# Two parts of the value weights split ahead of the copies of the transposed rows

## Chip, cores and metric

The kernel runs on one core of a Trainium2 chip. The metric is the device time of one execution in microseconds (us); the number given is the median of several executions, with the lowest and the highest beside it.

## What is computed

The input is a matrix of 2048 rows and 512 columns. Four layers follow each other, A, B, A, B. Each one normalizes its rows, projects them with weights of 512 by 512, applies an attention of 32 heads, projects the result back and adds it to its input. The change lies in the first layer A, at the very beginning of the program. Of its reference this matters:

```python
def _layernorm(x, axis=-1, eps=1e-5):
    m = jnp.mean(x, axis=axis, keepdims=True)
    v = jnp.var(x, axis=axis, keepdims=True)
    return (x - m) / jnp.sqrt(v + eps)
...
qkv = (x @ wqkv).reshape(B, S, 3, H, Dh)          # transposed to q, k, v
...
pq = jnp.einsum("bhsd,hdf->bhsf", q, w_phi)
pk = jnp.einsum("bhsd,hdf->bhsf", k, w_phi)
...
kv = jnp.einsum("bhsf,bhsd->bhfd", phi_k, v)
...
x = x + _A_ref(_layernorm(x, axis=-1), A_wqkv, A_w_phi, A_wo)
```

## The kernel before

**Splitting.** A float32 matrix is multiplied in three products of a faster type (fp32r). Each operand is cast to a high half (an ACT copy into a tile of type fp32r), and the low half is what the cast lost (a subtraction, raw minus high). A product is then high x high + high x low + low x high, three matmuls for each of the four parts of 128 that the inner dimension of 512 is cut into (`kc` = 0 to 3). `mm3` (L433) issues them, so one block of 128 rows by 512 columns takes 12 matmuls. In the profile, `w` is a tile of split weights (high or low), `hh` and `hl` are the high and low halves of the normalized and transposed rows, and `P` (tag P4) holds raw weights as loaded.

**The start.** `LayerA.first` (L648) works on the first 512 rows (four tiles of 128 rows, `t` = 0 to 3). It loads the raw key weights, the four row tiles, the raw value weights and the raw query weights, in this order, on SP's queue (`fetch`, L253, and `rows_of`, L393). While these land, PE transposes the key weights and folds `w_phi` into them (`folded`, L274). DVE takes the moments of the rows, and ACT and DVE normalize the tiles (L680 to L683): tiles 0 and 2 on ACT (`normal`), tiles 1 and 3 on DVE.

**The place of the change.** Then come, for each row tile, `columns` (L384): four PE transposes into a PSUM buffer of the tag g, an ACT copy to `hh`, and a DVE subtraction to `hl`. The tag g has four buffers (G = 4) that are taken in turn. After these, `next(upc[1])` issues the loads of the next 512 rows on SP into the four row tiles, which the transposes must have read. After that, for each part of the value weights, ACT casts the raw part to `vh` and `low` subtracts it on DVE (parts 0 and 2) or on POOL (parts 1 and 3). The same for the key weights follows, with all four subtractions on DVE. Then `v_tile` (L536) makes the values of the first row tiles: twelve matmuls for tile 0, twelve for tile 1, then the sixteen transposes of the query weights, then tiles 2 and 3.

```python
for t in range(4):
    columns(hT, t, xt[t])
upc = upcoming(1)
next(upc[1])
for kc in range(NC):
    act.copy(vh[:, kc, :], vraw[kc])
    low(pool if kc % 2 else dve, wv, kc, vraw[kc])
```

**What sets the order.** Each engine runs its instructions in order. The class `Ordered` (L144) ties every instruction of DVE, ACT, POOL and SP to the one written before it, and `held` (L164) does so for PE, so the program text is the order. An exception is marked by `loose`: the instructions of `prepare` (L297), which splits the weights of the later layers piece by piece and stores them, are tied to what stands before them, but nothing is tied to them. `run(p1[0], prepare())` (L1508) takes turns between the first pass of layer 1 and this preparation; `first` is run through before the preparation issues anything. Nearly all instructions carry the line of a helper (L154 for DVE, ACT, POOL and SP, L176 for matmuls, L180 for transposes), so they are told apart by the names of their tiles.

Of the kernel before, what the change touches and what calls it, by code (L numbers as in the profile page):

```python
# [20 lines left out]
NC = D // P  # L21
# [79 lines left out]
def interleave_kernel(ctx, tc, x_in, a_wqkv, a_wphi, a_wo, b_wq, b_wk, b_wv, b_wo, b_beta,  # L101
# [13 lines left out]
    def nm(s):  # L115
        uid[0] += 1
        return f"{s}_{uid[0]}"

    def T2(tag, bufs, dt=F32, shape=(P, 512)):
        return sp.tile(list(shape), dt, tag=tag, bufs=bufs, name=nm(tag))  # L120
# [41 lines left out]
    dve, act, pool, sync = [Ordered(e) for e in (nc.vector, nc.scalar, nc.gpsimd, nc.sync)]  # L162
# [51 lines left out]
    def wtiles(tag):  # L214
        if tag == "e8":
            return [T2("e8", 2 * NSET, F32R, (P, NC, D)) for _ in range(2)]
        return [wp.tile([P, NC, D], F32R, tag="w8", name=nm("w")) for _ in range(2)]

    def dtile(shape, name):
        return dr.tile(list(shape), F32, name=name)  # L220
# [32 lines left out]
    def fetch(src):  # L253

        raw = []
        for a in range(2):
            t = T2("P4", NP4, shape=(P, 2, D))
            sync.dma_start(out=t, in_=src[2 * a * P : 2 * (a + 1) * P, :].rearrange("(k p) n -> p k n", p=P))
            raw += [t[:, 0, :], t[:, 1, :]]
        return raw  # L260
# [13 lines left out]
    def folded(raw, chunks):  # L274


        wT = T2("e8", 2 * NSET, shape=(P, NC, D))
        for kc in range(NC):
            pt = PS("g", G)
            for c in range(NC):  # L280
                tp(pt[:, c * P : (c + 1) * P], raw[kc][:, c * P : (c + 1) * P], ident)
            act.copy(wT[:, :, kc * P : (kc + 1) * P], pt.rearrange("p (c x) -> p c x", c=NC))
            yield
        pf = PS("lg", 1, (P, 2, 512))
        pf = [pf[:, 0], pf[:, 1], PS("mx", 1), PS("my", 1)]
        for kc in range(NC):
            chunks.append(pf[kc])
            for c in range(NC):
                mm(chunks[kc][:, c * P : (c + 1) * P], lhsT=wT[:, c, kc * P : (kc + 1) * P],
                   rhs=phibd[:, c].rearrange("p h f -> p (h f)"), start=True, stop=True)  # L290
        yield
# [67 lines left out]
    def moments(st, t, x):  # L359
        bs = T2("bs", 2, shape=(P, 6))  # L360
        dve.bn_stats(bs, x)
        dve.bn_aggr(st[:, t, 0:2], bs)

    def guard(st):
        dve.tensor_scalar(st[:, :, 1], st[:, :, 1], 1e-5, None, op0=ADD)

    def root(st):
        act.activation(st[:, :, 3], st[:, :, 1], AF.Ln)
        act.activation(st[:, :, 2], st[:, :, 3], AF.Exp, scale=-0.5)

    def refine(st, eng):

        var, r, u = st[:, :, 1], st[:, :, 2], st[:, :, 3]
        eng.tensor_tensor(out=u, in0=r, in1=r, op=MUL)
        eng.tensor_tensor(out=u, in0=u, in1=var, op=MUL)
        eng.tensor_scalar(u, u, -0.5, 1.5, op0=MUL, op1=ADD)
        eng.tensor_tensor(out=r, in0=r, in1=u, op=MUL)
        eng.tensor_tensor(out=u, in0=st[:, :, 0], in1=r, op=MUL)
        eng.tensor_scalar(u, u, -1.0, None, op0=MUL)

    def normal(st, t, x):
        act.activation(x, x, AF.Identity, bias=st[:, t, 3:4], scale=st[:, t, 2:3])

    def columns(hT, t, x):  # L384
        pt = PS("g", G)
        for kc in range(NC):
            tp(pt[:, kc * P : (kc + 1) * P], x[:, kc * P : (kc + 1) * P], ident)
        pv = pt.rearrange("p (k t) -> p k t", k=NC)
        hv, lv = [h[:, :, t * P : (t + 1) * P] for h in hT]
        act.copy(hv, pv)  # L390
        wait(lambda: dve.tensor_tensor(out=lv, in0=pv, in1=hv.bitcast(F32), op=SUB))

    def rows_of(xsrc, s):  # L393
        xt = []
        for t in range(4):
            x = T2("x", 4)
            sync.dma_start(out=x, in_=xsrc[4 * s + t])
            xt.append(x)
        return xt

    def htiles(spare=None):
        if spare:
            return wtiles(spare)
        return [hp_.tile([P, NC, D], F32R, tag=tag, bufs=1, name=nm(tag)) for tag in ("hh", "hl")]
# [43 lines left out]
    def mm3_pair(one, two, kcs=range(NC), closed=True):  # L448

        terms = [(kc, a, b) for kc in kcs for a, b in ((0, 0), (0, 1), (1, 0))]  # L450
        half = len(terms) // 2
        parts = [(terms[:half], (one, two)), (terms, (two, one)), (terms[half:], (one, two))]
        steps = [(*term, sides, n == 0) for part, sides in parts for n, term in enumerate(part)]
        for step, (kc, a, b, sides, first) in enumerate(steps):
            ends = step == 0, step == len(steps) - 1
            for row, (po, lhs, rhs) in zip((0, 64), sides):
                i = mm(po, lhsT=lhs(a, kc)[row : row + 64], rhs=rhs(b, kc)[row : row + 64],
                       start=ends[0], stop=ends[1] and closed, tile_position=(row, 0))
                if first and step > 0 and row == 0:
                    after(i, passed)  # L460
            if step + 1 < len(steps) and steps[step + 1][4]:
                passed = sync.nop(nofuse=True)
                after(passed, i)
            if not ends[1]:
                yield
# [177 lines left out]
    class LayerA:  # L643
# [4 lines left out]
        def first(self, hT, vv, upcoming):  # L648

            wph = T2("U", 2)[:, 0 : NC * DH].rearrange("p (c f) -> p c f", c=NC)  # L650
            act.dma_start(out=ident, in_=c_ident)
            act.dma_start(out=bd, in_=c_bd)
            act.dma_start(out=wph, in_=a_wphi.rearrange("(c h) d f -> (h d) c f", c=NC))
            nc.scalar.preload_act_table_set("natural_log_exp_and_others")
            kraw = fetch(a_wqkv[:, D : 2 * D])
            xt = rows_of(self.xsrc, SEGS[0])
            vraw, qraw = [fetch(a_wqkv[:, i * D : (i + 1) * D]) for i in (2, 0)]
            st = T2("st", 2, shape=(P, 4, 8))
            hT[:] = htiles()
            (vh, vl), (kh, kl), (qh, ql) = wv, wk, wq = [wtiles(tag) for tag in ("w8", "w8", "e8")]  # L660
            for key, w in (("awv", wv), ("awk", wk), ("awq", wq)):
                kept[key] = [dtile((P, NC, D), nm(key)) for _ in range(2)]
                owed.extend(zip(kept[key], w))

            def low(eng, w, kc, raw):
                eng.tensor_tensor(out=w[1][:, kc, :], in0=raw, in1=w[0][:, kc, :].bitcast(F32), op=SUB)

            for c in range(NC):
                pool.tensor_tensor(out=phibd[:, c], in0=wph[:, c, :].unsqueeze(1).broadcast_to([P, 8, DH]),
                                        in1=bd[:, 16:24].unsqueeze(2).broadcast_to([P, 8, DH]), op=MUL)  # L670
            kf, qf = [], []
            kfold, qfold = folded(kraw, kf), folded(qraw, qf)
            for t in range(4):
                next(kfold)
                moments(st, t, xt[t])
            guard(st)
            root(st)
            refine(st, dve)
            next(kfold)
            normal(st, 0, xt[0])  # L680
            for t in (1, 3):
                dve.tensor_scalar(xt[t], xt[t], st[:, t, 2:3], st[:, t, 3:4], op0=MUL, op1=ADD)
            normal(st, 2, xt[2])  # L683
            for t in range(4):
                columns(hT, t, xt[t])
            upc = upcoming(1)
            next(upc[1])
            for kc in range(NC):
                act.copy(vh[:, kc, :], vraw[kc])
                low(pool if kc % 2 else dve, wv, kc, vraw[kc])  # L690
            for kc in range(NC):
                act.copy(kh[:, kc, :], kf[kc])
                low(dve, wk, kc, kf[kc])
            vt = v_tile(hT, wv, vv, ("g", G))
            for t in range(4):
                for _ in range(4):
                    next(vt)
                if t == 1:
                    for _ in range(4):
                        next(qfold)  # L700
                for _ in range(NEXT[t]):
                    next(upc[1])
            next(qfold)
            for kc in range(NC):
                act.copy(qh[:, kc, :], qf[kc])
                low(dve, wq, kc, qf[kc])
            return wq, wk, wv, upc
# [846 lines left out]
```

## Time and profile before

| what | value |
|---|---|
| median of three runs | 1360.74 us (1359.96 to 1362.49) |
| the profiled execution | 1361.73 us |
| its span in the trace | 1360.0 us |
| busy share of PE, DVE, ACT, POOL | 97%, 76%, 59%, 51% |
| granted PE clock, mean | 0.999 |
| PE's last transposes of the rows begin to end | 14.60 to 16.51 us |
| first value matmul | 17.85 us |
| transposes of the query weights begin | 26.14 us |

The span is the time from the first to the last thing that the trace shows; 1.73 us of the execution lie around it. Times in the trace count from the start of the span. A row of the timeline gives the start, the length from the first to the last of the instructions merged into it, the engine, the line, the operation with its tiles, and in brackets how long the engine was idle before it and what it was waiting for. Matmuls are pipelined: their recorded lengths overlap, so their distance, not their length, is their cost. In the names, `PE` is the matmul, `PEld` its weight load, and SP the queue that issues the loads.

### The profile page before, as it was taken

Reading aid. Unit: us, or ns where it says so; the run is one execution under the profiler, and the core shown is the slowest. Engines: PE = TensorE matmul, PEld = TensorE weight load, DVE = VectorE, ACT = ScalarE, POOL = GpSimd, SP = SyncE. Lnnn points to the kernel's source line nnn. Section 1 sums busy time; section 2 is a strip of 40 time slices with the busy share of each in tenths; the row PEclk is TensorE's granted clock in tenths of the full one; section 3 lists DMA queues with packets and bytes.
Section 4 is the critical chain, followed back from the end, with each engine's and each line's share of the span. In section 5 each row is a group of like instructions: output and inputs, shape, how many; then the busy total and the mean of one; then the engine's idle time right before and its main releaser. Section 6 shows DMA issues by size and latency. Waiting matters only on the chain.

```text
span 1360.0 us, 36811 instructions
## 1 busy us (share of the span) xinstructions
PE 1317.2 (97%) x14056; PEld 1028.9 (76%) x14056; DVE 1040.3 (76%) x3256; ACT 808.7 (59%) x1201; POOL 696.9 (51%) x1060
## 2 busy tenths in 40 slices
PE   7999989999999999999999998999999999999997
PEld 6888868777777877777768886786777787787764
DVE  4766778777888888888657677887778879878882
ACT  5556345547677677677544433453766866866654
POOL 1568666326447557345324356553356656654442
PEclk9999999999999999999999999999999999999999
DMA  6388447535654544546251103755555554544441
GB/s 205 102 325 278 157 132 231 173 97 140 173 167 131 158 117 134 153 120 182 87 181 37 63 33 126 241 164 132 143 163 164 152 157 99 150 130 98 118 116 42
DMA packets 134400, 196.27 MB, mean 144 GB/s; under 512 B 15440, under 2 KB 61648, under 8 KB 133456
## 3 DMA queue, kind: packets, MB, share of 16 engines
q1 hardware_dynamic: 132256, 193.27, 48.8%
q8 instruction: 112, 1.84, 0.6%
q10 hardware_dynamic: 1968, 0.64, 0.2%
q14 instruction: 64, 0.52, 0.1%
HBM read 101.05 MB, written 39.85 MB: 104 GB/s over the span
## 4 chain that ended last, share of the span: by engine, by line
PE 76%; DVE 11%; ACT 4%; issue 3%; POOL 3%; DMA 1%; SPq 0%; ACTq 0%; DVEq 0%; POOLq 0%
PE g L176 58%; PE lg L176 6%; PE g L180 6%; PE mx L176 3%; ACT P L154 2%; POOL P L154 2%; DVE g L154 2%; PE lg L180 2%; PE my L176 1%; DVE es L154 1%; POOL tb L154 1%; DVE my L154 1%; DVE mx L154 1%; DVE mxs L154 1%; PE mx L180 1%
## 5 line engine op out<-in xcount | busy, mean ns | idle before, releaser
L154 ACT ACTIVATE P<-lg 128x1024 f32<-128x1024 f32 x320 | 329.6, 1030 | 171.4 <-PE lg L176 93.8
L154 POOL TENSOR_SCALAR_AFFINE_SELECT P<-P 128x256 f32<-128x256 f32 (+1 forms) x448 | 193.4, 446 | 285.7 <-ACT P L154 284.0
L154 DVE CUSTOM_DVE_ANT_0 g<-g,mask 128x256 f32<-128x256 f32 (+3 forms) x392 | 191.6, 545 | 8.6 <-PE g L176 8.3
L176 PE MATMUL g<-hh,wqk 64*128 64x512 f32 (+1 forms) x960 | 186.5, 392 | 0.5 <-DMA wqk<-wqk 0.3
L176 PE MATMUL g<-w,oh 64*128 64x512 f32 (+2 forms) x880 | 177.7, 384 | 1.3 <-DVE ol L154 0.7
L154 DVE CUSTOM_DVE_ANT_0 mx<-mx,mask 128x512 f32<-128x512 f32 (+2 forms) x316 | 158.0, 500 | 21.3 <-PE my L176 17.6
L154 DVE CUSTOM_DVE_ANT_0 my<-my,mask 128x512 f32<-128x512 f32 (+2 forms) x316 | 164.1, 519 | 0.0
L176 PE MATMUL lg<-e,e 64*128 64x256 f32 (+2 forms) x1024 | 153.1, 339 | 4.1 <-ACT P L154 4.1
L176 PE MATMUL g<-P,v 128*32 128x128 f32 (+3 forms) x2064 | 151.1, 433 | 3.6 <-DVE mxs L154 3.0
L176 PE MATMUL g<-w,hh 64*128 64x512 f32 (+1 forms) x672 | 143.9, 395 | 2.0 <-ACT w L154 1.3
L154 DVE DVE_READ_ACCUMULATOR2_ANT mxs<- 128x1 f32 x1024 | 145.3, 142 | 0.0
L176 PEld LDWEIGHTS lg<-e,e 64*128 64x128 f32 x1024 | 102.1, 185 | 35.2 <-issue 11.3
L176 PEld LDWEIGHTS g<-P,v 128*32 128x32 f32 x2064 | 61.2, 109 | 87.5 <-issue 60.8
L176 PEld LDWEIGHTS g<-w,oh 64*128 64x128 f32 (+1 forms) x880 | 107.0, 186 | 18.5 <-SPq L154 3.0
L176 PEld LDWEIGHTS g<-hh,wqk 64*128 64x128 f32 (+1 forms) x960 | 105.6, 185 | 17.2 <-PE my L176 1.0
L154 POOL TENSOR_SCALAR tb<-tb 128x512 f32<-128x512 f32 x72 | 109.2, 1528 | 16.0 <-ACT tb L154 16.0
L176 PE MATMUL g<-w,ol 64*128 64x512 f32 (+2 forms) x440 | 115.6, 377 | 0.0
L176 PE MATMUL g<-hl,wqk 64*128 64x512 f32 (+1 forms) x480 | 106.2, 391 | 0.2
L176 PEld LDWEIGHTS g<-w,hh 64*128 64x128 f32 (+1 forms) x672 | 84.4, 187 | 16.1 <-ACT w L154 1.6
L154 ACT COPY tb<-g 128x512 f32<-128x512 f32 (+1 forms) x132 | 71.2, 576 | 42.7 <-PE g L176 40.8
L176 PE MATMUL g<-w,hl 64*128 64x512 f32 (+1 forms) x336 | 90.1, 392 | 0.0
L154 DVE TENSOR_REDUCE es<-P 128x64 f32<-128x1024 f32 x64 | 77.4, 1209 | 12.9 <-ACT P L154 12.9
(149 smaller groups left out, 2887.9 us busy)
## 6 DMA issues: line engine op xcount, KB each, us to landing
e<-ta SPq DMA_DIRECT2D x384, 128.0 KB
wqk<-wqk SPq DMA_DIRECT2D x128, 256.0 KB
x<-x SPq DMA_DIRECT2D x48, 256.0 KB
ot<-in SPq DMA_DIRECT2D x26, 256.0 KB
pq<-tb SPq DMA_DIRECT2D x24, 256.0 KB
tb<-pq SPq DMA_DIRECT2D x24, 256.0 KB
x<-xr SPq DMA_DIRECT2D x22, 256.0 KB
xr<-x SPq DMA_DIRECT2D x20, 256.0 KB
```

The source lines that it names most:

```text
L154: i = f(*a, **k)
L176: return held(nc.tensor.matmul(*a, **k))
L180: return held(nc.tensor.transpose(*a))
```

## The change

The loop over the four parts of the value weights becomes a function. It is called for parts 0 and 1 ahead of the four `columns`, and for parts 2 and 3 where the loop stood. Every instruction is still there, with the same operands and on the same engine. On ACT, the casts of parts 0 and 1 now stand ahead of the four copies to `hh`; on DVE, the subtraction of part 0 stands ahead of the four subtractions to `hl`; on POOL, the subtraction of part 1 stays the first of the two. The order on PE and SP is as it was.

```diff
             normal(st, 2, xt[2])
+            def split_v(kcs):
+                for kc in kcs:
+                    act.copy(vh[:, kc, :], vraw[kc])
+                    low(pool if kc % 2 else dve, wv, kc, vraw[kc])
+
+            split_v((0, 1))
             for t in range(4):
                 columns(hT, t, xt[t])
             upc = upcoming(1)
             next(upc[1])
-            for kc in range(NC):
-                act.copy(vh[:, kc, :], vraw[kc])
-                low(pool if kc % 2 else dve, wv, kc, vraw[kc])
+            split_v((2, 3))
             for kc in range(NC):
                 act.copy(kh[:, kc, :], kf[kc])
                 low(dve, wk, kc, kf[kc])
```

## The prediction

> **What bounds the kernel now.** I read the page first, for the engine that sets the span, then the chain of waits at the start of the run, where the change is.
>
> ```profile
> span 1360.0 us, 36811 instructions
> ...
> PE 1317.2 (97%) x14056; PEld 1028.9 (76%) x14056; DVE 1040.3 (76%) x3256; ACT 808.7 (59%) x1201; POOL 696.9 (51%) x1060
> ...
> PE 76%; DVE 11%; ACT 4%; issue 3%; POOL 3%; DMA 1%; SPq 0%; ACTq 0%; DVEq 0%; POOLq 0%
> ```
>
> PE is the bound almost everywhere, so time is won only where PE waits. The chain between 14 and 28 us (start, length, what) shows such a place:
>
> ```profile
> 14.76 0.45 PE g L180 x4
> ...
> 15.23 0.59 ACT hh L154
> ...
> 15.85 1.50 DVE hl L154 x3
> ...
> 18.25 0.69 DVE w L154
> ...
> 18.99 1.14 PE g L176 x3
> ...
> 20.13 6.17 PE g L176 x20
> 26.30 1.75 PE g L180 x16
> ```
>
> From 15.23 to 18.99 the end is set by ACT and DVE; after that only by PE. The timeline of the four engines (start, length, engine, operation, count, idle before it) tells who waits for whom:
>
> ```profile
> 12.37 1.52 ACT L154 ACTIVATE x<-x,st 128x512 f32<-128x512 f32 x2 [1.25 <-DVE st L154]
> 15.23 2.05 ACT L154 CAST hh<-g 128x512 fp32r<-128x512 f32 x4 [1.35 <-PE g L180]
> 17.15 2.21 ACT L154 CAST w<-P 128x512 fp32r<-128x512 f32 x4
> ...
> 12.37 1.00 DVE L154 TENSOR_SCALAR x<-x,st 128x512 f32<-128x512 f32 x2
> 15.85 2.49 DVE L154 TENSOR_TENSOR hl<-g,hh 128x512 fp32r<-128x512 f32 x4 [2.48 <-ACT hh L154]
> 18.25 2.37 DVE L154 TENSOR_TENSOR w<-P,w 128x512 fp32r<-128x512 f32 x2
> 20.55 0.68 DVE L154 TENSOR_TENSOR w<-lg,w 128x512 fp32r<-128x512 f32 x1
> ...
> 18.39 3.37 POOL L154 TENSOR_TENSOR w<-P,w 128x512 fp32r<-128x512 f32 x2 [8.13 <-ACT w L154]
> ...
> 14.60 1.91 PE L180 MATMUL g<-ident,x 128*128 128x128 f32 x16
> 17.85 0.49 PE L176 MATMUL g<-w,hh 128*128 128x512 f32 x1 [1.35 <-ACT w L154]
> 18.99 0.50 PE L176 MATMUL g<-w,hh 128*128 128x512 f32 x1 [0.64 <-DVE w L154]
> 19.32 0.40 PE L176 MATMUL g<-w,hl 128*128 128x512 f32 x1
> 19.56 1.37 PE L176 MATMUL g<-w,hh 128*128 128x512 f32 x2
> ```
>
> PE has its transposes done at 16.51, waits 1.35 us for the first cast of a value weight (v0 to v3 are the four parts) and 0.64 us for its low half. ACT is idle from 13.89 to 15.23 and DVE from 13.37 to 15.85; POOL has done nothing for 8.13 us.
>
> **Does a head start last?** The windows (length, then busy time of PE, PEld, DVE, ACT, POOL, then granted clock, DMA share, GB/s) answer it:
>
> ```profile
> 27.00:165.00 138.00, 138.00 (x1375) 113.35 (x1374) 92.97 (x153) 74.23 (x140) 95.44 (x115) 1.00 0.60 204
> ```
>
> PE is busy in all 138 us that follow, and the order on each engine is fixed in the code. What PE gains before 27 us should therefore arrive at 165 us whole, and from there the rest of the program shifts with it.
>
> **The clock is part of the price.** Four short windows frame the one place where the granted clock is not 1.00:
>
> ```profile
> 19.40:19.60 0.20, 0.20 (x3) 0.11 (x1) 0.20 (x1) 0.20 (x1) 0.20 (x1) 1.00 0.73 205
> 19.60:19.80 0.20, 0.20 (x2) 0.00 (x0) 0.20 (x1) 0.20 (x1) 0.20 (x1) 0.56 1.33 379
> ...
> 22.80:23.00 0.20, 0.20 (x2) 0.14 (x1) 0.20 (x1) 0.02 (x1) 0.00 (x0) 0.50 0.94 360
> 23.00:23.20 0.20, 0.20 (x3) 0.15 (x2) 0.20 (x2) 0.00 (x0) 0.00 (x0) 0.91 1.11 430
> ...
> 16.27:19.69 3.42, 1.43 (x7) 0.67 (x4) 3.42 (x6) 3.42 (x8) 1.30 (x1) 0.99 0.87 286
> ...
> 173.27:176.68 3.41, 1.98 (x9) 1.64 (x10) 2.67 (x5) 1.53 (x2) 2.11 (x3) 1.00 0.89 261
> ```
>
> The clock falls to one half at about 19.68 and is back by 23.03, some 3.4 us. In the 3.42 us before the fall PE was busy 1.43, or 42%. A stretch of that length with 1.98 (58%) kept its clock. So I take the fall to be the answer to PE's two waits.
>
> A matmul of 512 columns costs, at half and at full clock:
>
> ```profile
> 20.73 0.63 PE L176 MATMUL g<-w,hl 128*128 128x512 f32 x1
> ...
> 22.01 0.63 PE L176 MATMUL g<-w,hl 128*128 128x512 f32 x1
> ...
> 24.78 0.62 PE L176 MATMUL g<-w,hh 128*128 128x512 f32 x2
> ...
> 25.46 0.62 PE L176 MATMUL g<-w,hh 128*128 128x512 f32 x2
> ```
>
> The same place of the pattern of three returns after 22.01 - 20.73 = 1.28 us while slow (0.427 each) and after 25.46 - 24.78 = 0.68 us at full clock (0.227 each). Check on the kernel before: 20 matmuls from 20.13; until 23.05 there is room for 2.92/0.427 = 6.8, and 13.2 x 0.227 = 2.99 brings 26.04. The chain has 26.30: near enough, as I use differences.
>
> **The change, step by step.** It adds no instruction; two casts on ACT, one subtraction on DVE and one on POOL move ahead of eight instructions for the rows (four casts, four subtractions). No DMA or SP instruction moves, and the load of the next rows still waits for the same transposes.
>
> ```profile
> L154 ACT CAST w<-P x4: 647/648/652, 17.1 to 18.7; 128x512 fp32r<-128x512 f32 x4
> ...
> L154 DVE TENSOR_TENSOR w<-P,w x2: 681/1220/1758, 18.3 to 18.9; 128x512 fp32r<-128x512 f32 x2
> L154 POOL TENSOR_TENSOR w<-P,w x2: 1686/1708/1731, 18.4 to 20.0; 128x512 fp32r<-128x512 f32 x2
> ...
> 14.00:15.00 1.00, 1.00 (x11) 1.00 (x11) 0.00 (x0) 0.00 (x0) 0.00 (x0) 1.00 0.04 12
> ```
>
> (The first three rows give minimum, median and maximum in ns.)
>
> 1. Casts of v0 and v1: four start within 2.21 - 0.65 = 1.56 us, 0.52 apart, so two take 13.87 to 15.04. That is inside ACT's gap to 15.23, and the cast of the rows is not delayed. Their data: DMA moves almost nothing after 14.00 (12 GB/s), so the weights have landed by then. If v0's came last of all, the casts would end at 15.2, still no cost. If the gap were absent, they would cost 1.1 us.
> 2. Low half of v0 on DVE: 14.53 to 15.21, in the gap that lasts to 15.85. Nothing queued behind it waits; without the gap the rows' subtractions would come 0.68 later. Low half of v1 on POOL: 15.07 to 16.8 at most (1.73); POOL is idle there.
> 3. PE: the accumulator of the first product takes the PSUM buffer of the first rows, so it needs their subtraction, done at 15.85 + 0.68 = 16.53. Six matmuls (v0, v1) then run 16.57 to 17.93.
> 4. Casts of v2 and v3 take the places that v0 and v1 had: 17.15 and 17.67, ends 17.80 and 18.32. Low v2 on DVE runs 18.25 to 18.93, low v3 on POOL from 18.39, as v0 and v1 did before. The POOL result arrives at 20.07 (18.39 + 1.69).
> 5. So PE does v2's first matmul, waits from 18.16 to 18.99, does three, and goes on at 20.13 with v3's low half. At 20.13 it has 10 of 24 matmuls behind it, not 4: **14 are left, not 20**.
> 6. Clock: in 16.27 to 19.69 PE is now busy about 0.24 + 1.59 + 0.70 = 2.5 us, 74%, above the 58% that kept its clock. So I take no fall: 20.13 + 14 x 0.227 = 23.31 against 26.04, a gain of **2.73 us**. With the fall kept, the slow time holds the same 6.8 matmuls and the gain is 6 x 0.227 = 1.36 us.
>
> The later casts and subtractions of the key weights come some 1.5 us earlier; no one waits for them in this stretch.
>
> Sum: the profiled execution took 1361.73 (span 1360.0, 1.73 around it). 1361.73 - 2.73 = **1359.0**. The median of the three runs is 1360.74, so the gain to be seen against it is 1.7 us or 0.13%. Were the clock drop missing in the median run, its matmuls would end with POOL's last subtraction: 18.39 + 3.37 = 21.76, plus 14 x 0.227 is 24.94, 1.10 below 26.04, hence 1360.6. That fits the median but does not prove it.
>
> **Two rules beside the rows.** The Trainium skill, "TensorE: Matmul & The Clock Gate", section "What's actually happening", lets the clock fall only after a whole idle window of some 3.4 us. The length agrees with the 3.4 above, but PE idled 1.35 us at a time, so the measured fall disagrees. By that rule the changed kernel, whose waits are shorter, has no drop either, and the sum stays 1359.0; it speaks against the rival in which the slow clock stays, and could not explain the one measured. The Trainium skill, "SBUF — State Buffer", section "Who interferes with whom", says that a DVE instruction with two SBUF inputs and a reading GpSimd instruction exclude each other, whichever starts first. The trace agrees: DVE's second subtraction took 1758 ns beside POOL's first, while the one with a PSUM input took 0.68 us beside POOL.
>
> **Rivals.**
>
> - *POOL goes first.* In step 4 DVE leads POOL by 0.14 us. If POOL starts first and holds DVE off for about 1.15 us (18.93 to 20.07 is what the first POOL subtraction had to itself), low v2 is late instead of low v3: 17 matmuls are left at 20.13, 0.68 us more, 1359.7. For it: the small lead. Against: the same two slots went DVE first in the trace.
> - *The slow clock stays*, because 74% is not enough, or falls at another place: 1361.73 - 1.36 = 1360.4.
> - *The gain is given back* before 165 us, because the instructions of the weight preparation, free to move on ACT, POOL and SP, land badly: 1361.7. Against: PE had no idle moment there.
> - *Slower: the slow clock moves to two later places.* Two stretches lie as low as the one that fell, but their 3.4 us were cut differently:
>
> ```profile
> 179.00:182.41 3.41, 1.35 (x34) 1.22 (x35) 3.27 (x9) 1.80 (x2) 1.06 (x1) 1.00 0.02 5
> 833.50:836.91 3.41, 1.18 (x126) 1.07 (x114) 1.77 (x3) 2.40 (x3) 2.34 (x3) 1.00 1.03 372
> ```
>
> Busy 40% and 35%, both at clock 1.00. If a shifted program puts them whole into one measuring interval, each is followed by 3.4 us at half clock, at most 1.7 us each. One such drop leaves 1.0 of the gain (1360.7); both make it 3.4 - 2.73 = 0.7 slower than the profiled run, 1362.4. It decides from 2.73/1.7, so from the second drop.
>
> **Chances.** The measured runs spread from 1359.96 to 1362.49, so 0.2% (2.7 us) is about what a measurement can tell from no change: faster means below 1358.0, slower above 1363.5. Forecast 0.55 (1359.0, give or take 1.0); POOL first 0.07 (1359.7); slow clock stays or one drop elsewhere 0.17 (1360.4 to 1360.7); given back 0.08 (1361.7); slow clock at both places 0.13 (1362.4, more where such a drop also delays DVE's or ACT's work behind PE). The forecast is 1.0 above the line to faster. Runs that spread by 2.5 us reach over it in about two of five cases of the forecast (0.22) and in 0.03 of the others; of the last rival I count 0.10, of "given back" 0.02 as slower. Faster 0.25, same 0.63, slower 0.12. For the range I leave out the tenth of the chance at each end: below, the forecast less 1.6 (its 1.0 and half a spread's quarter of noise, 0.6), 1357.4; above, just short of the last rival, 1361.9.
>
> **What would show it.** Right: casts of v0 and v1 between 13.9 and 15.1 on ACT; the first value matmul near 16.6; waits of PE near 18.2 and 19.8 only; granted clock 1.00 through 23 us; the transposes of the query weights at about 23.4, not 26.1; 1357 to 1358 us of span. Wrong: rows cast after 15.3; a clock below 1.00 anywhere; PE idle between 24 and 162 us; low v2 over 1.2 us long.

## The result and the profile after

| | before | after |
|---|---|---|
| median of 21 runs each | 1362.24 us (1359.26 to 1365.63) | 1360.77 us (1356.71 to 1364.02) |
| ratio, after to before | | 0.9981, 95% interval 0.9973 to 0.9989 |
| profiled execution, span | 1361.73, 1360.0 us | 1362.60, 1360.8 us |
| mean granted clock of PE in that execution | 0.999 | 0.996 |

The change makes the kernel 0.19% faster (0.11 to 0.27%). The profiled execution of the changed kernel is nevertheless 0.87 us longer than that of the kernel before, so the two traces must be compared stage by stage, not by their ends.

By the shares of the chain of waits, the kernel as a whole is bound nearly as it was before (PE 76%, DVE 11%, ACT 4% then). After:

```profile
PE 75%; DVE 10%; ACT 5%; POOL 3%; issue 3%; DMA 3%; SPq 2%; ACTq 0%; DVEq 0%; POOLq 0%
```

The timeline after, in the stretch of the change. ACT first (start, length, what, idle before it):

```profile
12.63 1.52 ACT L154 ACTIVATE x<-x,st 128x512 f32<-128x512 f32 x2 [1.25 <-DVE st L154]
14.05 1.12 ACT L154 CAST w<-P 128x512 fp32r<-128x512 f32 x2
16.10 2.05 ACT L154 CAST hh<-g 128x512 fp32r<-128x512 f32 x4 [0.93 <-PE g L180]
18.02 1.17 ACT L154 CAST w<-P 128x512 fp32r<-128x512 f32 x2
```

DVE and POOL:

```profile
14.69 0.69 DVE L154 TENSOR_TENSOR w<-P,w 128x512 fp32r<-128x512 f32 x1 [1.05 <-ACT w L154]
16.72 2.49 DVE L154 TENSOR_TENSOR hl<-g,hh 128x512 fp32r<-128x512 f32 x4 [1.34 <-ACT hh L154]
19.12 0.68 DVE L154 TENSOR_TENSOR w<-P,w 128x512 fp32r<-128x512 f32 x1
...
15.25 1.27 POOL L154 TENSOR_TENSOR w<-P,w 128x512 fp32r<-128x512 f32 x1 [4.67 <-ACT w L154]
19.27 1.68 POOL L154 TENSOR_TENSOR w<-P,w 128x512 fp32r<-128x512 f32 x1 [2.74 <-ACT w L154]
```

PE:

```profile
15.47 1.91 PE L180 MATMUL g<-ident,x 128*128 128x128 f32 x16
17.47 0.74 PE L176 MATMUL g<-w,hh 128*128 128x512 f32 x2
...
19.86 0.50 PE L176 MATMUL g<-w,hh 128*128 128x512 f32 x1 [0.48 <-DVE w L154]
...
21.00 0.50 PE L176 MATMUL g<-w,hh 128*128 128x512 f32 x1 [0.18 <-POOL w L154]
...
24.32 1.91 PE L180 MATMUL g<-ident,P 128*128 128x128 f32 x16
```

The casts of v0 and v1 lie in ACT's gap, with 0.93 us of it left. PE's waits for v0's cast (1.35 us) and v0's low half (0.64) are gone; it now waits for v2's low half (0.48) and v3's (0.18). From the start of the row transposes to the start of the query-weight transposes (called **D** below) it takes 24.32 - 15.47 = 8.85 us, before 26.14 - 14.60 = 11.54: **2.69 us less**. But the row transposes themselves began 0.87 us later in this execution, so in the trace's own time the gain is 26.14 - 24.32 = 1.82.

The gain is then carried on, as the windows of after say (PE busy in all of 138 us again):

```profile
27.00:165.00 138.00, 138.00 (x1371) 113.22 (x1370) 93.82 (x153) 73.90 (x139) 95.26 (x115) 1.00 0.61 210
```

Where it goes is seen in the chain of waits at the start of the second pass. Before:

```profile
184.46 4.16 PE g L176 x44
...
190.65 4.16 PE g L176 x44
```

After:

```profile
182.50 6.80 PE g L176 x44
...
191.34 4.16 PE g L176 x44
```

The same 44 matmuls begin 1.96 us earlier and take 2.64 us longer; the next ones begin 0.69 us later than before. The windows of after give the reason in the last but two column, the granted clock:

```profile
178.10:181.51 3.41, 1.37 (x16) 1.25 (x12) 3.27 (x10) 0.07 (x1) 1.64 (x2) 1.00 0.02 5
180.10:183.51 3.41, 2.67 (x30) 2.30 (x32) 3.34 (x7) 1.98 (x3) 2.18 (x3) 0.71 0.00 0
183.51:186.92 3.41, 3.41 (x26) 2.82 (x23) 1.58 (x5) 0.58 (x1) 3.09 (x3) 0.50 0.03 7
186.92:190.34 3.42, 3.42 (x19) 2.92 (x18) 1.00 (x2) 0.07 (x1) 0.00 (x0) 0.79 0.00 0
```

PE was busy 1.37 of 3.41 us (40%), and then ran at half clock from 181.5 to 188.4. A second fall follows in the second layer A; the same twelve matmuls, before and after:

```profile
836.88 3.06 PE L176 MATMUL g<-e,w 128*128 128x512 f32 x12
839.77 1.03 PE L180 MATMUL lg<-ident,P 128*128 128x128 f32 x8
```

```profile
837.38 4.38 PE L176 MATMUL g<-e,w 128*128 128x512 f32 x12
841.60 1.04 PE L180 MATMUL lg<-ident,P 128*128 128x128 f32 x8
```

After is 0.50 late at the first row and 1.83 late at the second. A lag is not passed on whole either: by the starts of the same ACT instructions it is 1.82 us at 851 us, but 0.89 at 1000 us, and the spans differ by 0.8. So the profiled execution is the rival in which the slow clock moves to two later places: 1362.60, where the prediction had 1362.4 for it.

### The profile page after: what moved, and what is told of

Its sections match the earlier page's. It is cut to its first block, busy times and chain, and to the rows that moved or that the text cites. A ratio compares the mean times of both kernels' runs of the same rounds, so it can differ in the third digit from the quotient of the medians.

```text
span 1360.8 us, 36810 instructions
## 1 busy us (share of the span) xinstructions
PE 1319.7 (97%) x14056; PEld 1033.7 (76%) x14056; DVE 1039.1 (76%) x3256; ACT 808.1 (59%) x1201; POOL 694.9 (51%) x1060
## 4 chain that ended last, share of the span: by engine, by line
PE 75%; DVE 10%; ACT 5%; POOL 3%; issue 3%; DMA 3%; SPq 2%; ACTq 0%; DVEq 0%; POOLq 0%
PE g L176 56%; PE lg L176 6%; PE g L180 6%; PE mx L176 3%; ACT P L154 2%; PE lg L180 2%; DVE g L154 2%; SPq L154 2%; POOL P L154 1%; PE my L176 1%; POOL tb L154 1%; DMA x<-x 1%; DVE es L154 1%; PE mx L180 1%; DVE my L154 1%
## 5 line engine op out<-in xcount | busy, mean ns | idle before, releaser
L154 DVE DVE_READ_ACCUMULATOR2_ANT mxs<- 128x1 f32 x1024 | 142.5, 139 | 0.0
```

Of the source, the lines that this page charges most:

```text
L154: i = f(*a, **k)
```

## The experiments

Theory: **slots**. Each part of the value weights that is ready early takes one wait away; PE then has the matmuls left that it had not done when the last low half arrives, at 0.227 us each. The avoided fall of the clock is a second, smaller part of the gain. Rivals: ACT is the bound, so that what is moved ahead comes back as delay of the rows; or it was the clock alone. Two measures are used: D as above, and M, from the start of the rows' normalization on ACT (12.37 before, 12.63 after) to the same end, so 13.77 before and 11.69 after.

### One, three and four parts ahead

```diff
-            split_v((0, 1))
+            split_v((0,))
...
-            split_v((2, 3))
+            split_v((1, 2, 3))
```

This is the edit of the first (e1). The second (e2) calls it for parts 0, 1 and 2 and then for 3, the third (e3) for all four and then for none.

> Only part 0 of the value weights is moved ahead of the rows; parts 1 to 3 stay behind. D is the time from the start of the row transposes to the start of the query-weight transposes: 11.54 us before, 8.85 after. Theory (slots: each part that is ready early takes its wait away, and PE then does what is left at 0.227 us a matmul): the low half of v1 arrives near 19.0 and that of v3 near 20.7 in the times of the trace before, 14 matmuls are left then, D about 9.5 at full clock, up to 10.5 if the clock falls to half (PE is busy near 53% of the critical 3.4 us). Rival (it was the clock alone: any kernel without the fall gains alike): D 10.4 without the fall, 11.5 with it.

> Parts 0, 1 and 2 ahead of the rows, low halves of 0, 2 and 3's turn as before (0 and 2 on DVE, 1 and 3 on POOL). Theory (slots, with DVE and POOL excluding each other when both read two SBUF operands): casts fill ACT's gap and 0.2 us more, the low half of v2 on DVE is held by POOL's v1 until about 16.4, the rows' subtractions start about 1.0 later than before, but PE then never waits again: D about 8.5. Without the exclusion D about 8.0. Rival (ACT is the bound, whatever is moved ahead beyond its gap comes back as delay of the rows): D 9.0 or more, worse than the 8.85 of the change.

> All four parts ahead of the rows. Theory (slots): the rows' casts are about 0.7 us late, but the rows' subtractions are held by DVE's v2 just as with three parts ahead, so D is the same, about 8.5. Rival (ACT is the bound): the fourth cast adds its 0.5 us, D 9.5.

e1, PE:

```profile
15.54 1.91 PE L180 MATMUL g<-ident,x 128*128 128x128 f32 x16
...
18.80 0.51 PE L176 MATMUL g<-w,hh 128*128 128x512 f32 x1 [0.29 <-ACT w L154]
20.15 0.50 PE L176 MATMUL g<-w,hh 128*128 128x512 f32 x1 [0.85 <-POOL w L154]
...
25.21 1.03 PE L180 MATMUL g<-ident,P 128*128 128x128 f32 x8
```

D is 25.21 - 15.54 = 9.67, and the clock did not fall here: the theory's 9.5, not the 10.4 of the clock alone. The waits are those for v1's cast and v1's low half, as they should be (one execution took 1361.67).

e2, DVE, POOL and PE:

```profile
15.91 1.34 DVE L154 TENSOR_TENSOR w<-P,w 128x512 fp32r<-128x512 f32 x1 [0.34 <-ACT w L154]
...
15.43 1.27 POOL L154 TENSOR_TENSOR w<-P,w 128x512 fp32r<-128x512 f32 x1 [5.16 <-ACT w L154]
...
13.68 1.97 PE L180 MATMUL g<-ident,x 128*128 128x128 f32 x16 [0.18 <-ACT x L154]
17.90 0.74 PE L176 MATMUL g<-w,hh 128*128 128x512 f32 x2 [2.26 <-DVE hl L154]
...
23.50 1.91 PE L180 MATMUL g<-ident,P 128*128 128x128 f32 x16
```

In this execution the clock was released early, the row transposes began 0.87 us after the normalization (2.23 in the trace of before, 2.84 after), and D (9.82) is no fair measure. M is 10.69, which is the theory's 8.5 plus 2.23; the rival's 9.0 or more would be 11.2 or more. That does not decide between them, though: the changed kernel itself, with an equally early start (e7, below), has M 10.66. Beside it, e2 has its row copies 0.5 us later and its first value matmul 1.28 us later after the normalization (5.09 against 3.81), and saves just as much behind. So the third part won nothing in this form: what it saves comes back as delay of the rows, 0.5 us of it on ACT, as the rival has it, and 0.8 on DVE, where v2's low half now stands ahead of the rows and is held up by POOL. DVE's second subtraction took 1.34 us instead of 0.68, because POOL's was under way. The Trainium skill, "SBUF — State Buffer", section "Who interferes with whom", says that a DVE instruction with two SBUF inputs contends with a GpSimd instruction that reads SBUF, and that the order of issue decides which of them is blocked. Here POOL was first: 15.43 + 1.27 = 16.70, and 16.70 to 17.25 is what DVE had left. e3 did the same up to there (first value matmul 5.10 us after the normalization), with the same wait of 2.26 us on PE, but its clock fell from 19.2 to 22.7 us, and e2's did not: M 12.28. The wait alone thus does not decide; the last section has a likely reason. So the prediction of "no difference" held for the waits and failed for the end. (One execution each: 1360.59 and 1365.65.)

### Three parts ahead, low halves of parts 1 and 2 on POOL

```diff
-                    low(pool if kc % 2 else dve, wv, kc, vraw[kc])
+                    low(pool if kc in (1, 2) else dve, wv, kc, vraw[kc])
...
-            split_v((0, 1))
+            split_v((0, 1, 2))
```

> Parts 0, 1 and 2 ahead, and the low halves of parts 1 and 2 on POOL, those of 0 and 3 on DVE, so that DVE has one subtraction ahead of the rows and POOL's two lie beside the rows' subtractions, which read only one SBUF operand. Theory (slots): rows' subtractions 0.2 us late, low v3 on DVE right behind them near 19.1, no wait of PE after the first matmul: D about 7.9, one us below the change's 8.85; end to end that is 0.07%, hardly to be seen, so ratio to before about 0.9975 (2.7 + 1.0 us, less what the clock does elsewhere). Rival (ACT is the bound): D about 9, ratio 0.998 to 0.999.

```profile
15.31 1.91 PE L180 MATMUL g<-ident,x 128*128 128x128 f32 x16
17.31 0.73 PE L176 MATMUL g<-w,hh 128*128 128x512 f32 x2
...
22.99 1.91 PE L180 MATMUL g<-ident,P 128*128 128x128 f32 x16
```

No row of PE in between has a wait: D is 7.68, 1.17 us below the change (forecast 7.9). The ratio to before is 0.998 (0.9968 to 0.9993), median 1359.19 of 12 runs beside 1361.67: a version at least as good as the change, but not to be told from it end to end.

### Is it the wait or the clock?

```diff
             for t in range(4):
                 columns(hT, t, xt[t])
+            filler = PS("g", G)
+            for n in range(8):
+                tp(filler[:, n % 4 * P : (n % 4 + 1) * P], ident, ident)
```

> The kernel before, with eight extra transposes of the identity on PE behind the row transposes, into a PSUM buffer that nobody reads: 0.9 us of work in the wait for the first cast of a value weight, nothing else. PE's busy share of the critical 3.4 us goes from 42% to about 67%. Theory (the gain has two parts, waits 1.6 us and the avoided fall of the clock 1.1 us): no fall before 24 us, D about 10.4. Rival (the fall hangs on the waits as such, or on something else than PE's share): the clock falls as before, D 11.5.

```profile
15.45 1.91 PE L180 MATMUL g<-ident,x 128*128 128x128 f32 x16
17.45 1.09 PE L180 MATMUL g<-ident 128*128 128x128 f32 x8
18.71 0.51 PE L176 MATMUL g<-w,hh 128*128 128x512 f32 x1 [0.16 <-ACT w L154]
19.84 0.51 PE L176 MATMUL g<-w,hh 128*128 128x512 f32 x1 [0.63 <-DVE w L154]
...
20.99 0.50 PE L176 MATMUL g<-w,hh 128*128 128x512 f32 x1 [0.17 <-POOL w L154]
...
25.99 1.91 PE L180 MATMUL g<-ident,P 128*128 128x128 f32 x16
```

No fall before 24 us, and D is 10.54. The order is that of before, so 11.54 - 10.54 = **1.00** us was the fall, and 10.54 - 8.85 = **1.69** the waits. The rows show it directly. In all three kernels v3's low half lets PE go on 5.53 to 5.54 us after the start of the row transposes (20.13, 20.99 and 21.00 on the clocks of the three traces). Behind that point the kernel before had 20 matmuls left, which took 6.01 us with the fall; e5 had the same 20, in 5.00; the changed kernel had 14, in 3.32. This is the cleanest result of the study, with one execution of each: useless work on PE won 1 us in this stretch. (This one execution took 1362.06; it had a fall at 181 to 185 us instead.)

### The same kernels again

Before (e0) and after (e12), unchanged, with one execution each (1360.88 and 1361.24).

> The kernel before, unchanged, a second look. D is the time from the start of the row transposes to the start of the query-weight transposes. Theory (PE's two waits bring the clock down, and the measuring intervals are cut differently in each execution): D 11.5 if the clock falls between 16 and 24 us, 10.3 to 10.4 if it does not; the later falls lie elsewhere than in the first look. Rival (the fall belongs to the program and always comes at the same place): one fall only, at 19.7 to 23.0, D 11.5, as in the first look.

> The changed kernel, unchanged, a second look. M is the time from the start of the rows' normalization on ACT to the start of the query-weight transposes. Theory: M between 10.7 (row transposes 0.9 us after the start of the normalization) and 11.7 (2.8 us after), against 12.75 and 13.8 for the kernel before; no fall of the clock between 16 and 24 us; the later falls are not where the first look had them (181.5 and 836.9 us from the start), or only in part, because each execution cuts the measuring intervals differently. Rival (the change itself moves the falls to these two places): falls at 181.5 and 836.9 again.

Before again: the clock fell at 19.5 to 22.9 us, and once more at 835.3. The rows' transposes began at 13.68, 0.91 us after the normalization:

```profile
13.68 1.93 PE L180 MATMUL g<-ident,x 128*128 128x128 f32 x16
16.95 0.50 PE L176 MATMUL g<-w,hh 128*128 128x512 f32 x1 [1.34 <-ACT w L154]
...
25.52 1.91 PE L180 MATMUL g<-ident,P 128*128 128x128 f32 x16
```

D is 11.84, above the 11.5 expected, because ACT had no gap: its row copies waited for the normalization, not for PE. M is 12.75, so the same kernel's start differs by 1.0 us between two executions. After again: D 8.85, to the hundredth what it was, M 11.49, no fall before 24 us; later falls at 181, at 836 and, new, at 1327 us. Two of three places were those of the first trace, which speaks for the rival. Over all traces, the eight that kept the clock in the first 24 us all have a fall between 177 and 189 us (the version below with fillers there left out), and of the five that lost it early two do. That an early fall protects from the late one is thus suggested, not shown. Over many runs the balance is about even: mean granted clock 0.9972 in 51 runs of before, 0.9975 in 21 of after (not run at the same time).

### Only the casts ahead

```diff
-            def split_v(kcs):
+            def split_v(kcs, cast):
                 for kc in kcs:
-                    act.copy(vh[:, kc, :], vraw[kc])
+                    if cast:
+                        act.copy(vh[:, kc, :], vraw[kc])
+                        continue
                     low(pool if kc % 2 else dve, wv, kc, vraw[kc])
...
-            split_v((0, 1))
+            split_v((0, 1), True)
...
-            split_v((2, 3))
+            split_v((2, 3), True)
+            split_v((0, 1, 2, 3), False)
```

> The changed kernel, but only the casts of parts 0 and 1 (ACT) stand ahead of the rows; all four subtractions are issued behind the rows' ones. POOL has nothing ahead of its own, so v1's still runs early; DVE's v0 comes behind the rows' four. D (row transposes to query-weight transposes) is 8.85 after the change, 11.5 before. Theory (slots): PE does one value matmul, then waits about 2.2 us for v0's low half, with 23 matmuls left: D about 9.7 at full clock; the wait brings the clock down as in the kernel before, which makes it 10.5 to 10.9. Rival (the casts on ACT are what counts, DVE's place is free): D 8.9.

```profile
13.52 1.94 PE L180 MATMUL g<-ident,x 128*128 128x128 f32 x16
16.41 0.51 PE L176 MATMUL g<-w,hh 128*128 128x512 f32 x1 [0.96 <-DVE hl L154]
18.81 0.50 PE L176 MATMUL g<-w,hh 128*128 128x512 f32 x1 [1.89 <-DVE w L154]
...
25.78 0.49 PE L180 MATMUL g<-ident,P 128*128 128x128 f32 x3
```

One matmul, then 1.89 us of idle PE for v0's low half, and the clock fell at 19.4. D itself is 12.26, far above the 10.5 to 10.9 expected, but the row transposes began early again (0.91 us after the normalization). M is 13.17, just above the 12.7 to 13.1 that the expected D makes of it with 2.23; the rival's 8.9 would be 11.1. The order of before had M 12.75 with the same early start and the clock fallen too (e0). So without a gap on ACT the casts alone win nothing, and lose 0.4; the gain needs DVE's early subtraction too. An execution of this version with the gap was not traced. (One execution: 1360.04.)

### Without the slow start: is the gap in ACT real cover?

```diff
+            dve.memset(mask[:, 0:P], 1.0)
+            warm = PS("g", G)
+            for n in range(16):
+                mm(warm[:, n % 4 * P : (n % 4 + 1) * P], lhsT=mask[:, 0:P], rhs=mask[:, 0:P], start=True, stop=True)
```

The matmuls stand ahead of the first loads' use, in the kernel before (e9), the changed one (e7) and the one with three parts ahead (e10).

> The kernel before, with 16 extra matmuls of 128 columns at the very start (on a tile set to one), while PE waits for the first loads, so that the slow clock of the start is over before 9 us. M is the time from the start of the rows' normalization on ACT to the start of the query-weight transposes: 13.77 before, 11.69 after the change. Theory (PE's slow start, not the normalization, sets when the rows are transposed, and opens ACT's gap): row transposes begin 0.9 us after the start of the normalization, not 2.2, M 12.4 with the fall of the clock at 16 to 24 us and 11.3 without; ACT's gap in front of the row copies is gone. Rival (the start is set by loads, the clock there does not matter): M stays 13.8.

> The changed kernel with the same 16 extra matmuls at the start, so that the rows are transposed some 0.9 us after the start of their normalization and ACT has no gap ahead of the row copies. M (start of the normalization to start of the query-weight transposes) was 11.69 after the change with a late release of the clock, and 12.85 and 12.75 in the order of before with an early one (clock fallen at 19 to 23 us). Theory (the two casts now delay the row copies by about 1 us, but two of four waits are gone): row copies begin 2.5 us after the start of the normalization, M 10.7 without a fall. Rival (the cover does not matter): M 9.8. Rival (without the gap the casts cost what they save): M 11.7 or more.

> The version with three parts ahead (low halves of parts 1 and 2 on POOL) and the 16 extra matmuls at the start. Theory (slots): row copies 3.0 us after the start of the normalization, no wait of PE after the first value matmul, M 10.0; against M 12.75 to 13.8 before some 3.2 us, ratio 0.997 to 0.998, no better than the same version without the extra matmuls by more than 0.5 us. Rival (with the gap gone, ACT is the bound and the third cast costs): M 10.7 or more, ratio 0.9985 or more.

e7, ACT and PE:

```profile
15.16 2.03 ACT L154 CAST hh<-g 128x512 fp32r<-128x512 f32 x4
...
13.67 1.91 PE L180 MATMUL g<-ident,x 128*128 128x128 f32 x16
...
23.36 1.91 PE L180 MATMUL g<-ident,P 128*128 128x128 f32 x16
```

| kernel | row transposes, us after N | M | forecast of M | clock in the first 24 us |
|---|---|---|---|---|
| before | 2.23 | 13.77 | | falls |
| before again (e0) | 0.91 | 12.75 | | falls |
| before, warm (e9) | 1.03 | 12.85 | 12.4 | falls |
| after | 2.84 | 11.69 | | stays |
| after, warm (e7) | 0.97 | 10.66 | 10.7 | stays |
| three ahead (e4) | 2.79 | 10.47 | 10.1 | stays |
| three ahead, warm (e10) | 1.00 | 10.03 | 10.0 | stays |

(N is the start of the normalization; e4's forecast is its D of 7.9 plus 2.23.) The two with parts ahead hit, e9 is 0.45 above its forecast. So the slow start opens ACT's gap, and where it is gone the two casts delay the rows' copies, from 1.57 us after N (e0) to 2.46 (e7). Still the change wins 12.85 - 10.66 = 2.19 us there. Some 1.3 of that is the avoided fall (the last 20 matmuls ahead of the query weights took 6.28 us in e9 and 5.00 in e5), so about 0.9 is left for the waits, against 1.69 where ACT has its gap.

End to end the extra matmuls won nothing: e10 is at 1.000 (0.999 to 1.0009), where 0.997 to 0.998 was expected. Its twelve runs all have a mean clock of 0.994 to 0.997 (0.9959 on average, against 0.9967 for the 17 runs of before beside them), those of e4 from 0.994 to 1.000, and its trace has falls at 179 to 186 and 835 to 838 us. So M was won, and part of it lost again to the clock elsewhere: at the same clock (below) e10 is some 1.1 us ahead of before, where M alone would make it about 2.8. Why its clock is low in every run, and where the rest goes, is open. (e7 and e9, one execution each: 1364.89 and 1361.75.)

### Against the late falls

```diff
+                for q in range(5 if i == 1 else 0):
+                    tp(pt[:, 0, q % 4 * P : (q % 4 + 1) * P], ident, ident)
...
+                    for q in range((8, 5, 5, 5)[i] if i < 4 and half == 0 else 0):
+                        tp(pn[:, 0:P], ident, ident)
```

> The version with three parts ahead (low halves of parts 1 and 2 on POOL), and in both layers A five to eight extra transposes of the identity ahead of PE's waits at the start of the second pass (near 179 to 196 us and 841 to 860 us), into PSUM that the real work overwrites afterwards. Theory (falls of the clock cost most of what the change wins): no fall between 177 and 188 us, where five of six traces so far have one that costs up to 2.6 us; ratio to before 0.996 to 0.997, median 1357 to 1358. Rival (falls there are hidden behind ACT and POOL, or the extra work delays PE as much): ratio stays at 0.998.

In the profiled execution the falls are gone: the clock was at full speed but for the last microseconds, where PE has nothing to do. But the ratio is 0.9999 (0.999 to 1.0009; median 1361.93): **this part of the theory failed.** One reason is that other runs still have falls somewhere: of the twelve only two have a mean clock of 1.000, the rest 0.995 to 0.999, and their mean, 0.9979, is hardly above e4's 0.9975. Another shows in the trace. By the starts of the same ACT instructions, its profiled execution is 3.2 us ahead of e4's at 852 us and only 1.05 at 1240. PE twice waits about 0.5 us for SP (1056.8 and 1236.9 us), where it has no such wait in e4; SP is held there by long issues of the loads of the key and query weights of the second layer B (minimum, median and maximum of one issue, in e6 and then in e4):

```profile
L154 SPq DMA_DIRECT2D wqk<-wqk x60: 360/522/2109, 911.4 to 1264.2; - x60
```

```profile
L154 SPq DMA_DIRECT2D wqk<-wqk x60: 359/502/597, 914.6 to 1266.0; - x60
```

One issue held SP for 2.1 us. The fillers need not be the cause: the traces of before and after, which have none, show issues of this group of up to 2.06 and 1.82 us. Where the rest of the lead went was not followed up.

### What the change is worth at the same clock

The mean clock is known, to 0.001 (1.4 us), for 51 runs of the kernel before, for the 21 of the changed one, and for 36 of e4, e6 and e10. The 51 were run beside the experiments, not beside the 21; for the 21 runs of before in the result no clock was recorded. A straight line through all of them (one level for each kernel, one slope on the microseconds of lost clock, which comes out as 0.69 us per lost us) puts the changed kernel **1.68 us below before, give or take 0.61** (95%), and e4 2.13 +/- 0.75. e10 lies 1.06 +/- 0.78 below, and e6 0.46 +/- 0.76 above.

## Why the prediction was right, and where not

1. **Casts in ACT's gap** (step 1): right, 14.05 to 15.17 with 0.93 us left. What the prediction took as given, the gap itself, changes with each execution: 0.9 to 2.8 us from the normalization to the row transposes. Its forecast of "1.1 us where the gap is absent" was about right: the row copies come 0.89 us later (2.46 against 1.57). One sign that it had named for being wrong, rows cast after 15.3, was seen (16.10), but here PE's late transposes set that time, not the casts.
2. **DVE and POOL** (steps 2 and 4): right. v0's low half 0.69, v1's 1.27 (at most 1.73 was allowed), DVE ahead of POOL by 0.15 us for v2 and v3 (0.14 forecast). "POOL goes first" did not happen in the three traces with the change's order (after, e12, e7); e2 shows what it costs.
3. **14 matmuls left, not 20** (step 5): right, with the last low half as late as before (5.53 us after the start of the row transposes in both). From 21.00 to 24.32 they took 3.32 us, against 14 x 0.227 = 3.18.
4. **No fall of the clock** (step 6): right. D fell by 2.69 (2.73 forecast). e5 splits it into 1.69 of waits (1.63) and 1.00 of clock (1.10). The changed order kept the early clock in three traces of three (after, e12, e7), the order of before lost it in three of three (before, e0, e9). The reason given, a share of 74% against a safe 58%, was only roughly right: PE is busy at least 2.7 of any 3.41 us in the two traces of the change (80%), and 1.97 (58%) in e7 with its early start, but other falls came after 62 and 63%. The rule that the clock falls only after a wholly idle window (the Trainium skill, "TensorE: Matmul & The Clock Gate", "What's actually happening") is again not what the traces show: 40% busy before the fall at 181.5. That the window runs freely of the kernel, as the same section says, fits the 0.9 to 2.8 us of step 1 and the spacing of the falls (last section).
5. **A head start lasts to 165 us**: right, 1.82 at 24 us and 1.96 at 184 us.
6. **From there the program shifts as a whole**: this step failed as it was put. The falls of the clock behind it are as dear as the gain (2.64 and 1.33 us in the profiled execution), and both traced executions of the changed kernel have them. "A clock below 1.00 anywhere" was a sign that the prediction had named for being wrong, and its span of 1357 to 1358 us became 1360.8. It had this case as a rival with 0.13, priced at 0.7 above the profiled run; measured 0.87. That the total fits so well is partly luck: the first fall lasted 6.85 us and cost 2.64, not 3.4 us and at most 1.7, and 0.9 of the lag was made up later. As the mean clocks are about equal, what is left on average should be the waits' part: 1.68 give or take 0.61 measured at the same clock, 1.63 forecast. The interval, 1.07 to 2.29, is wide, and where ACT has no gap the waits' part is only about 0.9, so the size is confirmed only roughly.
7. **The time**: 1360.77, within the range, 1.8 above 1359.0. Of that, 0.5 is the start of the sum: it began at one execution, 1361.73, where the median of 21 is 1362.24. The other 1.3 is the gain, 2.73 forecast and 1.47 measured by medians: the whole 2.73 was subtracted as if the clock could be kept elsewhere. The median of before that three runs gave, 1360.74, was low, and that it fitted a run without an early fall was chance. Against the measured 1362.24 the gain is 1.47 by medians and 2.6 by the ratio, so within 0.2% as forecast, just.

## What to carry to other kernels

Find the stretch in which the bound engine waits, list what it still has to do when the last late operand arrives, and count instructions: that gave D or, where the row transposes began early, M to half a microsecond here wherever the clock was foreseen rightly. Put work ahead only where an engine has a gap, and ask whether the gap belongs to the program or to the execution. A gain of two microseconds in a kernel whose clock falls now here, now there is seen in the trace at once, and end to end only over some twenty runs, best at equal clock.

## What was not expected of the hardware

- The slow start is not in the clock column, which reads 1.00 from the beginning, but only in the durations. The groups by shape of the kernel before (after the bar busy us and mean ns of one), from 4.5 to 10 us and from 14 to 17 us:

```profile
L180 PE MATMUL g<-ident,P 128*128 128x128 f32 x16 | 3.6, 423 | 4.9 <-DMA P<-in 4.9
...
L180 PE MATMUL g<-ident,x 128*128 128x128 f32 x16 | 1.9, 272 | 0.0
```

  The same transposes of 128 columns take 423 ns first and 272 later.
- Each execution has its own grid of intervals. Wherever a trace holds more than one fall, their starts lie a whole number of times 3.413 us apart: 192.0 times in the trace after (181.52 and 836.88), 47.0 and 240.0 times in e3 (19.23, 179.65 and 838.43).
- This fits e2 and e3. Counted back from its fall at 180.74, the grid of e2 cuts PE's wait in two, and PE is busy 1.97 and 2.41 of the two 3.41 us; in e3 the wait lies in one interval with 1.51, and the fall follows. It also bears on the two stretches of before with 40% and 35% that the prediction feared: counted from the fall at 19.62, the grid there has intervals of 66% and more.
- On these grids the share of busy time ahead of a fall was 33 to 50% for 23 of 25 falls (those of the last 3 us left out), but 62 and 63% for one each in e11 (1326.7 us) and e12 (1327.7). Three intervals with 43 to 47% (in e0 and e11) kept their clock. So the recorded share is a good guide, not a threshold.
